# Prefix sums as rows of the second score product, pairs split at once, and a first batch in plain float32 products

## The chip, the cores and the metric

The kernel runs on one core of a Trainium2 chip. The metric is the device time of one execution in microseconds (us). Five engines matter: PE (TensorE, which multiplies; its weight loads are shown apart, as PEld), DVE (VectorE), ACT (ScalarE), POOL (GpSimd) and SP, which here only issues DMA transfers. Each engine takes its instructions strictly in the order in which the program has them.

## The reference

A forgetting attention feeds a channel mix. All is float32; 8 batches, 8 heads, 576 positions, 64 values a head.

```python
scores = q @ k.T / sqrt(64)
cum    = cumsum(maximum(s, 0))
bias   = -(cum[:, None] - cum[None, :])
scores = where(causal, -1e9, scores + minimum(bias, 0))
attn   = softmax(scores)
x      = attn @ v                      # heads side by side: 512 values a position
xk, xr = mix of x and the position before, by mu_k and mu_r
out    = sigmoid(xr @ w_r) * (relu(xk @ w_k) ** 2 @ w_v)
```

A row's own cumulated sum is the same for the whole row and falls out of the softmax, so the kernel adds only the sum of the key's position to a score.

## The kernel before, in words

**Products.** PE multiplies float32 operands at the rate of a rounded form (fp32r). To keep accuracy each operand is split in a high part (a cast by ACT) and a low part (a subtraction by POOL or DVE). For the scores, G holds the high part of q in rows 0 to 63 and the low part in rows 64 to 127; KH holds the high part of k twice, KL the low part twice. Two products into one PSUM bank, G by KH and G by KL, then hold all four partial products (line 689). For the values the weights are split in ph and pl and V holds high and low parts side by side (line 944); the two halves of the result are put together by ACT and DVE (lines 974 and 978).

**Tiles.** A head's queries come in five tiles: tile 0 of 64 queries and tiles 1 to 4 of 128, which see 64, 192, 320, 448 and 576 keys. For each tile: the two products, then DVE's pass at line 704, which adds the bias and scales, writes W and keeps the running minimum nm (one instruction and a read of its accumulator for each piece), then ACT's exponentials with their sums (722), POOL's division (736), transposes on PE (783, 797), and the split of the transposed weights (823 to 887). The bias of a tile comes from CB, a copy of the head's prefix sums on all 128 partitions that a DMA brings (629), and for the diagonal block from M, which POOL makes out of CB by an affine_select that puts -1e9 above the diagonal (649). So a tile's pass is cut at the diagonal block: a head of all five tiles has 10 pieces.

**Stages.** Heads are worked in pairs (a visit). Batch 0 is visited in two rounds: first tiles 0 to 2 of its four pairs (A), then tiles 3 and 4 (Z); the other batches take all five tiles in a visit (ALL). The result xT of a visit goes to DRAM (x_d, line 1272). The channel mix takes 256 positions of it at a time (a chunk, 36 in all, loaded at line 1173): lines 1020 to 1052 mix and split, 1081 and 1148 are the two large products, 1123 the gate. The weights arrive in float64 and are taken apart by ACT, DVE and POOL in the first 120 us (lines 506 to 537).

**Order.** A planner writes the order: every instruction is a task with an engine, a cost, what it depends on and a due time; `Plan.forward` puts them in a list for each engine. Loads of the next visit are due LEAD = 1.85 steps ahead, its split (`prepare`) 0.17 of a step behind the start of the visit before. Until the first value product, PE fills pauses with products of the identity (line 359). The change leaves the due times of the visits and chunks as they are; the order of nearly every engine is new all the same, since it comes out of the costs.

Of the kernel before, what the change touches and what calls it, by code (L numbers as in the profile page):

```python
# [285 lines left out]
def forgetting_attention_then_channel_mix(  # L286
# [15 lines left out]
    nc = tc.nc  # L302
# [94 lines left out]
    def zero(t):  # L397
        for kb in range(NQ - 1):
# [12 lines left out]
    cum_d = fixed(dram.tile([B * H, S], F32, name="cum_d"))  # L411

    def prefix_sums():
        cum = sbuf([B * H, S], "mask", 2)
        spos = sbuf([B * H, S], "mask", 2)
        ones = sbuf([B * H, S], "raw", 4)
# [19 lines left out]
        dma(lambda: nc.sync.dma_start(cum_d.ap, cum.get()), [cum], [cum_d], 410)  # L436

    def first_sums(nk):

        raw = sbuf([P, 2, nk], "raw", 4)  # L440
        ones = sbuf([P, nk], "raw", 4)
        cbs = [sbuf([P, nk], "cb", 2) for _ in range(2)]
        dma(
            lambda: nc.sync.dma_start(raw.get(), s[0:1, 0:2, 0:nk].broadcast_to([P, 2, nk])),
            [], [raw], 819 * 2 * nk / S,
        )
        pool(lambda: nc.gpsimd.memset(ones.get(), 1.0), [], [ones], nk, 36)
        act(
            lambda: nc.scalar.activation(raw.get(), raw.get(), AF.Relu, scale=ISCALE),
            [], [raw], 2 * nk, 94,  # L450
        )
        for j in range(2):
            dve(
                lambda j=j: nc.vector.tensor_tensor_scan(
                    out=cbs[j].get(), data0=ones.get(), data1=raw.get()[:, j], initial=0.0,
                    op0=ALU.mult, op1=ALU.add,
                ),
                [ones, raw], [cbs[j]], 2 * nk,
            )
        return cbs  # L460

# [83 lines left out]
    first = []  # L545
# [26 lines left out]
    def load_turned(src, b, hp, a, e, tag, plain):  # L572

        if plain:
            x = sbuf([P, e - a], tag, 3)
            dma(
                lambda: nc.sync.dma_start(
                    x.get(), src[b, 2 * hp : 2 * hp + 2, :, a:e].rearrange("h d t -> (h d) t")
                ),
                [], [(x, 0), (x, 1)], 819 * (e - a) / S,  # L580
            )
            return [x]
        xs = [sbuf([P, e - a], "raw", 4) for _ in range(2)]
        for j in range(2):
            for r in range(2):
                dma(
                    lambda j=j, r=r: nc.sync.dma_start(
                        xs[j].get()[64 * r : 64 * r + 64], src[b, 2 * hp + j, :, a:e]
                    ),
                    [], [(xs[j], r)], 410 * (e - a) / S,  # L590
                )
        return xs

    def split_qk(qs, ks):

        nq, nk = qs[0].n, ks[0].n
        G = [sbuf([P, nq], "G", 3, F32R) for _ in range(2)]
        KH, KL = ([sbuf([P, nk], x, 3, F32R) for _ in range(2)] for x in ("KH", "KL"))
        for j in range(2):
            k, kh, kl = ks[j], KH[j], KL[j]  # L600
            act(
                lambda k=k, kh=kh: nc.scalar.copy(kh.get(), k.get()),  # L602
                [(k, 0), (k, 1)], [(kh, 0), (kh, 1)], nk, 150,
            )
            pool(
                lambda k=k, kh=kh, kl=kl: nc.gpsimd.tensor_tensor(  # L606
                    out=kl.get(), in0=k.get(), in1=f32(kh.get()), op=ALU.subtract
                ),
                [(k, 0), (k, 1), (kh, 0), (kh, 1)], [(kl, 0), (kl, 1)], nk, 114, 2.21,
            )  # L610
            q, g = qs[j], G[j]
            act(
                lambda q=q, g=g: nc.scalar.copy(g.get(), q.get()),
                [(q, 0), (q, 1)], [(g, 0), (g, 1)], nq, 150,
            )
            pool(
                lambda q=q, g=g: nc.gpsimd.tensor_tensor(  # L617
                    out=g.get()[64:P], in0=q.get()[64:P], in1=f32(g.get()[64:P]), op=ALU.subtract
                ),
                [(q, 1)], [(g, 1)], nq, 114, 2.21,  # L620
            )
        return G, KH, KL

    def scores(b, h, tiles, G, KH, KL):

        NK = KN[tiles[-1]]
        CB = sbuf([P, NK], "cb", 2) if not first else first.pop(0)
        (b == 0 and h < 2 and tiles == A) or dma(
            lambda: nc.sync.dma_start(
                CB.get(), cum_d.ap[b * H + h : b * H + h + 1, 0:NK].broadcast_to([P, NK])  # L630
            ),
            [cum_d], [CB], 819 * NK / S,
        )
# [7 lines left out]
        M = sbuf([P, S], "mask", 2)  # L641

        def mask(m, k0, n):
            def own(x):
                x = x.get()[:m, k0 : k0 + n * m]
                return x if n == 1 else x.rearrange("p (t x) -> p t x", x=m)

            pool(
                lambda: nc.gpsimd.affine_select(
                    out=own(M),  # L650
                    in_=own(CB),
                    pattern=[[-1, m]] if n == 1 else [[0, n], [-1, m]],
                    base=0,
                    channel_multiplier=1,
                    compare_op=ALU.is_ge,
                    fill=MASK * ISCALE,
                ),
                [CB], [(M, k0 > 0)], n * m, 137,
            )

        def halved(t, a, x):
            return x.rearrange("p (k x) -> p k x", x=64) if lead(t) and a >= QS[t] else x

        def placed(t, a, e, x):
            if not lead(t):
                return x[:, a:e]
            if a < QS[t]:
                return x[:, 64 + a : 64 + e]
            x = x[:, : KN[t] // 64 * 64].rearrange("p (k x) -> p k x", x=64)
            return x[:, KN[t] // 64 - 1 :: 1 - KN[t] // 64]  # L670

        def products(t, m, i, k0, w, W):
            ps = bank(1, "s", 2)
            q0 = QS[t] - QS[tiles[0]]
            if KL is None:
                r = slice(64 * (h % 2), 64 * (h % 2) + 64)
# [3 lines left out]
                        G.get()[r, q0 : q0 + m],  # L680
                        KH.get()[r, k0 : k0 + w],
# [3 lines left out]
                    [(G, x) for x in range(2)] + [(KH, x) for x in range(2)], [ps], w, m, 4 / 2.4, 64,  # L685
                )
            for x, K in enumerate((KH, KL) if KL is not None else ()):
                pe(
                    lambda x=x, K=K: nc.tensor.matmul(  # L689
                        ps.get()[:m, :w],  # L690
                        G.get()[:, q0 : q0 + m],
                        K.get()[:, k0 : k0 + w],
# [3 lines left out]
                    [(G, x) for x in range(2)] + [(K, x) for x in range(2)], [ps], w, m,  # L696
# [651 lines left out]
```

## Time and profile before

| | us |
|---|---|
| median of 3 runs | 919.47 (918.21 to 920.49) |
| profiled execution | 918.27 |
| its span | 916.5 |
| PE busy | 861.8 (94%) |
| DVE busy | 714.7 (78%) |
| ACT busy | 702.1 (77%) |
| POOL busy | 519.1 (57%) |

The span is the time from the first to the last instruction. Busy shares are means over stages that differ: in the first 140 us the other engines are as full as PE, and PE's granted clock, 1.00 at 2.4 GHz, is lower there. PE's busy time counts each product up to its modelled end, and products overlap, so the pace of PE is read from starts.

### The profile page before, as it was taken

What the parts mean: (1) busy time and instruction counts of PE and PEld (TensorE: products, weight loads), DVE (VectorE), ACT (ScalarE), POOL (GpSimd) and SP (SyncE); (2) the same over time, 40 slices, a digit from 0 to 9 for tenths busy, and PEclk for the clock granted to TensorE, in tenths of its full rate; (3) what the DMA queues carried; (4) which work ended last, traced back from release to release, by engine and by line L of the source; (5) the groups of instructions that cost most, each with busy time, mean ns of one, the idle gap of its engine ahead of it and who ended that gap; (6) DMA issues with size and microseconds to landing.
All of it is one profiled execution on the core that took longest, in us unless ns stands there. A gap on an engine that the chain in (4) does not pass through costs nothing. (4 is left out here: it accounts for less than half of the span.)

```text
span 916.5 us, 18293 instructions
## 1 busy us (share of the span) xinstructions
PE 861.8 (94%) x5354; PEld 746.7 (81%) x5354; DVE 714.7 (78%) x2537; ACT 702.1 (77%) x1906; POOL 519.1 (57%) x880
## 2 busy tenths in 40 slices
PE   6778789999999999999999999999999999998998
PEld 4557667877888888897989898989798979888886
DVE  5998998988988888788878888888887877546431
ACT  5888888989998889688978888888787977445331
POOL 6998788698776566666663747564566552100000
PEclk7568979999999999999999999999999999999999
DMA  7788835446355342534342525242435220101100
GB/s 207 219 230 253 237 99 170 115 133 181 112 149 166 104 146 87 145 105 154 111 140 86 158 92 154 76 146 86 139 105 152 80 74 25 41 31 35 47 24 24
DMA packets 65044, 110.87 MB, mean 121 GB/s; under 512 B 10544, under 2 KB 26416, under 8 KB 64944
## 3 DMA queue, kind: packets, MB, share of 16 engines
q1 hardware_dynamic: 64944, 109.71, 40.5%
q8 instruction: 42, 0.69, 0.3%
q14 instruction: 58, 0.48, 0.2%
HBM read 90.64 MB, written 19.04 MB: 120 GB/s over the span
## 5 line engine op out<-in xcount | busy, mean ns | idle before, releaser
L1081 PE MATMUL m<-xh,w_k 128*128 128x256 f32 x1152 | 231.4, 286 | 2.8 <-DVE kl L1110 2.5
L722 ACT ACTIVATE W<-W,nm 128x448 f32<-128x448 f32 (+4 forms) x320 | 179.7, 562 | 44.0 <-DVE nm L704 40.8
L1148 PE MATMUL m<-w_v,kh 128*128 128x512 f32 x576 | 197.4, 400 | 0.0
L1081 PEld LDWEIGHTS m<-xh,w_k 128*128 128x128 f32 x1152 | 186.4, 190 | 5.2 <-DVE kl L1110 3.1
L736 POOL TENSOR_SCALAR W<-W,rinv 128x192 f32<-128x192 f32 (+4 forms) x320 | 165.4, 537 | 19.3 <-DVE rinv L766 17.4
L1081 PE MATMUL m<-xl,w_k 128*128 128x256 f32 x576 | 163.1, 283 | 0.0
L689 PE MATMUL s<-KH,G 128*128 128x288 f32 (+4 forms) x384 | 124.8, 333 | 19.0 <-DVE nm L704 13.9
L617 POOL TENSOR_TENSOR G<-raw,G 64x576 fp32r<-64x576 f32 (+2 forms) x72 | 93.1, 1293 | 76.3 <-issue 50.8
L825 DVE TENSOR_TENSOR pl<-t,ph 128x256 fp32r<-128x256 f32 (+3 forms) x264 | 120.1, 475 | 12.7 <-ACT ph L823 10.3
L606 POOL TENSOR_TENSOR KL<-raw,KH 128x576 fp32r<-128x576 f32 (+1 forms) x72 | 98.6, 1371 | 49.4 <-ACT KH L602 45.0
L783 PE MATMUL t<-ident,W 128*128 128x128 f32 x640 | 117.4, 285 | 8.2 <-POOL xT L1288 2.7
L1148 PEld LDWEIGHTS m<-w_v,kh 128*128 128x128 f32 x576 | 107.2, 189 | 17.7 <-ACT g L1135 0.2
L689 PE MATMUL s<-KL,G 128*128 128x288 f32 (+4 forms) x384 | 117.3, 308 | 1.1 <-POOL KL L606 1.1
L1029 DVE SCALAR_TENSOR_TENSOR xp<-x,mu,xp 128x256 f32<-128x256 f32 (+3 forms) x192 | 80.8, 421 | 45.9 <-ACT xp L1020 42.5
L944 PE MATMUL po<-ph,V 128*128 128x448 f32 (+4 forms) x344 | 106.9, 325 | 9.4 <-ACT ph L823 5.4
L823 ACT CAST ph<-t 128x256 fp32r<-128x256 f32 (+3 forms) x264 | 103.9, 417 | 14.3 <-PE t L783 6.0
L1148 PE MATMUL m<-w_v,kl 128*128 128x512 f32 x288 | 114.2, 397 | 0.0
L1081 PEld LDWEIGHTS m<-xl,w_k 128*128 128x128 f32 x576 | 109.2, 190 | 1.2 <-DVE xl L1052 0.4
L1020 ACT ACTIVATE xp<-x,mu 128x256 f32<-128x256 f32 (+3 forms) x192 | 81.4, 424 | 33.2 <-DVE xl L1052 11.1
L689 PEld LDWEIGHTS s<-KH,G 128*128 128x128 f32 (+1 forms) x384 | 72.3, 189 | 41.4 <-DVE nm L704 26.9
L704 DVE CUSTOM_DVE_ANT_0 W<-s,cb 128x64 f32<-128x64 f32 (+3 forms) x256 | 95.1, 376 | 11.6 <-PE s L689 9.9
L1123 PE MATMUL m<-w_r,xh 128*128 128x512 f32 x288 | 101.4, 407 | 0.1
(100 smaller groups left out, 1825.5 us busy)
## 6 DMA issues: line engine op xcount, KB each, us to landing
raw<-in_k SPq DMA_DIRECT2D x128, 144.0 KB, 3.1
cb<-cum_d SPq DMA_DIRECT2D x64, 288.0 KB, 3.8
raw<-in_q SPq DMA_DIRECT2D x112, 144.0 KB, 3.3
vn<-in_v SPq DMA_DIRECT2D x32, 320.0 KB, 3.4
out<-g SPq DMA_DIRECT2D x36, 256.0 KB, 2.4
x_d<-xT SPq DMA_DIRECT2D x28, 288.5 KB, 2.7
x<-x_d SPq DMA_DIRECT2D x12, 514.0 KB, 4.4
w_k<-in_moe_w_k SPq DMA_DIRECT2D x8, 512.0 KB, 5.2
```

The costliest lines, as they stand in the source:

```text
L606: lambda k=k, kh=kh, kl=kl: nc.gpsimd.tensor_tensor(out=kl.get(), in0=k.get(), in1=f32(kh.get()), op=ALU.subtract),
L689: lambda x=x, K=K: nc.tensor.matmul(ps.get()[:m, :w], G.get()[:, q0 : q0 + m], K.get()[:, k0 : k0 + w], start=x == 0, stop=x == 1,),
L704: lambda a=a, e=e, bias=bias, i=i: nc.vector.tensor_tensor_reduce(out=placed(t, a, e, W.ap[:m]), in0=halved(t, a, ps.get()[:m, a - k0 : e ...
L722: lambda: nc.scalar.activation(W.ap[:m, :n], W.ap[:m, :n], AF.Exp, bias=nm.get()[:m, 3 * t + mi : 3 * t + mi + 1], scale=-1.0, accum_out=s ...
L736: lambda: nc.gpsimd.tensor_scalar(out=to, in0=W.ap[:m, :n], scalar1=rinv.get()[:m, t : t + 1], scalar2=1.0, op0=ALU.mult, op1=ALU.mult,),
L783: lambda: nc.tensor.transpose(ps.get()[0:m, place : place + P], pt[t].ap[:, lead(t) + k0 : lead(t) + k0 + m], ident.ap),
L823: act(lambda: nc.scalar.copy(strips(ph), src()), [ps], [(ph, k) for k in ks], n * m)
L825: lambda: nc.vector.tensor_tensor(out=strips(pl), in0=src(), in1=f32(strips(ph)), op=ALU.subtract),
L944: lambda: nc.tensor.matmul(po.get()[: P if both else 64, at + q0 - base : at + q0 - base + m], V.get()[:, kb, 2 * j : 2 * j + (2 if both e ...
L1081: lambda u=u, f=f, c=c, n=n, w=w, x=x: nc.tensor.matmul(ps.get()[:, u * CT : (u + 1) * CT], weight["k", c, f // 4].get()[:, w, f % 4 * P : ...
L1123: lambda c=c, n=n, x=x, w=w: nc.tensor.matmul(ps.get(), x.get()[:, c, ts], weight["r", c, 0].get()[:, w], start=c == 0 and n == 0, stop=c ...
L1148: lambda f=f, n=n, x=x, w=w: nc.tensor.matmul(ps.get(), x.get()[:, f, ts], weight["v", f, 0].get()[:, w], start=f == 0 and n == 0, stop=f ...
```

## The change

**Batch 0.** `PLAIN = 8` makes its eight visits plain: q and k are loaded pair-wise as they are (`load_plain`) in rows 0 to 63, row 64 of k's tile gets the prefix sums and row 64 of q's a one, and one float32 product of 65 rows gives scores with their bias. V is not split, the weights are not split, one float32 product of 128 rows stands for two, and ACT alone copies the result.

**The other batches.** The prefix sums are cut in three fp32r pieces and put in rows 64 to 66 of KL, beside the low part of k in rows 0 to 63; the rest is zero. The second product has its own stationary operand, G2: the high part of q (a DMA copies it from G), three rows of ones, zeros. The first product is the old one. What CB and M did is now in the product, but for the mask, which is one constant tile (`causal`) for all heads. A tile's pass is cut only where its result is put in another order (tiles 2 and 4) and where a tile has two banks (tile 4): 8 pieces instead of 10. The second product gives up low q by low k.

**Pairs.** q and k of both heads are loaded and split by one instruction each.

```diff
+    def constant_rows():
+        for x in KLs + G2s:
+            dve(lambda x=x: nc.vector.memset(f32(x.get()[64:P]), 0.0), [], [(x, 1)], S)
+        for x in G2s:
+            dve(lambda x=x: nc.vector.memset(f32(x.get()[64 : 64 + PIECES]), 1.0), [], [(x, 1)], S)
...
+        dma(lambda: nc.sync.dma_start(whole_d.ap, cum.get()), [cum], [whole_d], 410)
+        first_cum.append(cum)
+        load(0)
+        plan.due = 15000.0
+        for i in range(PIECES):
+            dve(
+                lambda i=i: nc.vector.tensor_copy(sums_of_s.get()[:, i], cum.get()),
+                [cum], [(sums_of_s, i)], S,
+            )
...
+                    lambda j=j: nc.sync.dma_start(
+                        x.get()[64:65, j], first_cum[0].get()[row + j : row + j + 1, a:e]
+                    ),
...
+            dma(
+                lambda: nc.sync.dma_start(
+                    f32(KL.get()[64 : 64 + PIECES, :, 0:nk]),
+                    cum_d.ap[row : row + 2, :, 0:nk].rearrange("h p t -> p h t"),
+                ),
+                [cum_d, (KL, 1)], [(KL, (j, 2)) for j in range(2)], 520,
+            )
...
+                dma(
+                    lambda: nc.sync.dma_start(f32(G2.get()[0:64, :, 0:nq]), f32(G.get()[0:64])),
+                    part(G, 0), part(G2, 0), 819 * nq / S,
+                )
...
-        CB = sbuf([P, NK], "cb", 2) if not first else first.pop(0)
-        (b == 0 and h < 2 and tiles == A) or dma(
-            lambda: nc.sync.dma_start(
-                CB.get(), cum_d.ap[b * H + h : b * H + h + 1, 0:NK].broadcast_to([P, NK])
-            ),
-            [cum_d], [CB], 819 * NK / S,
-        )
...
-            if KL is None:
-                r = slice(64 * (h % 2), 64 * (h % 2) + 64)
+            if G2 is None:
                 pe(
                     lambda: nc.tensor.matmul(
                         ps.get()[:m, :w],
-                        G.get()[r, q0 : q0 + m],
-                        KH.get()[r, k0 : k0 + w],
+                        G.get()[0:65, h % 2, q0 : q0 + m],
+                        KH.get()[0:65, h % 2, k0 : k0 + w],
                         start=True,
                         stop=True,
                     ),
...
-            for a, e in ((k0, min(k0 + w, QS[t])), (max(k0, QS[t]), k0 + w)):
+            n = KN[t]
+            for a, e in ((k0, min(k0 + w, n - lead(t))), (max(k0, n - lead(t)), k0 + w)):
...
-                        in1=halved(t, a, bias.get()[:m, a:e]),
+                        in1=causal.get()[:m, S - P - QS[t] + a : S - P - QS[t] + e],
...
-        if 0 in tiles:
-            mask(64, 0, 1)
-        mask(P, QS[max(1, tiles[0])], len([t for t in tiles if t]))
...
+            if plain:
+                return
             dve(
                 lambda: nc.vector.tensor_tensor(
                     out=strips(pl), in0=src(), in1=f32(strips(ph)), op=ALU.subtract
                 ),
...
-    PLAIN, PLAINQ = 0, 0
+    PLAIN = 8
...
-    nc = bacc.Bacc("TRN2", target_bir_lowering=False, num_devices=1)
+    nc = bacc.Bacc("TRN2", target_bir_lowering=False, num_devices=1, dynamic_dma_scratch_size=1024)
```

Three places in the order of the program show what moves. PE in the early round of batch 0 before: value products of one head (po, by ph and pl), with the score products (s) of another head, two of each.

```order
L944 MATMUL po_87<-ph_103,V_174 128x320
L944 MATMUL po_87<-pl,V_174 64x320
L944 MATMUL po_87<-ph_103,V_174 128x192
L944 MATMUL po_87<-pl,V_174 64x192
L944 MATMUL po_87<-ph_103,V_174 128x64
L689 MATMUL s_205<-KH_276,G_248 128x320
L689 MATMUL s_205<-KL_288,G_248 128x320
L944 MATMUL po_87<-pl,V_174 128x64
```

The same engine and round after:

```order
L975 MATMUL po_93<-ph_120,V_217 128x320
L975 MATMUL po_93<-ph_120,V_217 128x192
L975 MATMUL po_93<-ph_120,V_217 128x64
L827 MATMUL t_313<-ident,W_72 128x128
L723 MATMUL s_203<-KH_190,G_102 128x320
L723 MATMUL s_201<-KH_190,G_102 128x192
```

One product in float32 stands where two in fp32r stood; the transposes (t) are what they were.

DVE in a head of all five tiles before: tiles 1 to 3 of the score pass (the rows with W; each is followed by the read of its accumulator), each in a piece with cb and one with mask (tile 3's second reads as tile 1's).

```order
L704 ISA W_72,nm_267<-s_208,cb_158 128x64
...
L704 ISA W_72,nm_267<-s_208,mask_105,nm_267 128x128
...
L704 ISA W_72,nm_267<-s_205,cb_158 128x192
L704 ISA nm_267 128x1
L704 ISA W_72,nm_267<-s_205,mask_105,nm_267 128x2x64
...
L704 ISA W_72,nm_267<-s_208,cb_158 128x320
```

The same tiles after:

```order
L751 ISA W_72,nm_232<-s_203,causal 128x192
L751 ISA nm_232 128x1
...
L751 ISA W_72,nm_232<-s_201,causal 128x256
...
L751 ISA W_72,nm_232<-s_201,causal,nm_232 128x64
...
L751 ISA W_72,nm_232<-s_203,causal 128x448
```

Tiles 1 and 3 have one piece instead of two, tile 2 still has two.

SP in the later batches after: the pieces of the sums (KL), the copy of q's high part (G into the second operand), and what is queued behind.

```order
L653 DMA KL_79<-cum_d 3x2x576
L1220 DMA x_649<-x_d_84 128x4x257
L635 DMA raw_97<-in_k 64x2x576 x2
L1324 DMA x_d_85<-xT_128 128x577
L576 DMA vn_867<-in_v 128x640
L698 DMA G_81<-G_819 64x1152
L635 DMA raw_99<-in_q 64x2x576 x2
```

Two loads of cb on 128 partitions for each pair are gone from this queue.

## Rows read from the trace of the kernel before

**Rows 1.** Windows by stage: length, busy us (instructions) of each engine, granted clock, DMA.

```profile
core 0: us, PE busy (x) PEld busy (x) DVE busy (x) ACT busy (x) POOL busy (x), PEclk, DMA share, GB/s
...
10.90:69.70 58.80, 43.20 (x169) 30.54 (x170) 51.81 (x197) 46.56 (x147) 53.53 (x97) 0.57 0.77 221
69.70:139.60 69.90, 59.08 (x334) 48.94 (x333) 64.85 (x207) 60.41 (x151) 58.38 (x76) 0.85 0.68 197
139.60:300.00 160.40, 152.34 (x1002) 131.08 (x1001) 140.76 (x562) 144.47 (x414) 122.50 (x210) 1.00 0.50 144
300.00:800.00 500.00, 490.95 (x3186) 435.47 (x3186) 403.71 (x1481) 403.36 (x1106) 279.33 (x474) 1.00 0.37 110
```

**Rows 2.** Timeline of SP, first two chunk loads: start, us, what.

```profile
69.73 0.59 SPq L1173 DMA_DIRECT2D x<-x_d  x1
...
140.24 0.56 SPq L1173 DMA_DIRECT2D x<-x_d  x1
```

**Rows 3.** Timeline of PE in the middle, two products back to back.

```profile
423.41 0.40 PE L1148 MATMUL m<-w_v,kl 128*128 128x512 f32 x1
423.64 0.62 PE L1148 MATMUL m<-w_v,kh 128*128 128x512 f32 x2
```

**Rows 4.** Timeline of PE in the early round.

```profile
31.88 0.47 PE L689 MATMUL s<-KH,G 128*128 128x320 f32 x1
32.15 0.47 PE L689 MATMUL s<-KL,G 128*128 128x320 f32 x1
...
33.47 0.69 PE L783 MATMUL t<-ident,W 128*128 128x128 f32 x2
33.95 0.42 PE L797 MATMUL t<-ident,W 128*128 128x128 f32 x1
```

**Rows 5.** Groups of DVE, 0 to 139.6 us: busy us, mean ns, idle before.

```profile
L825 DVE TENSOR_TENSOR pl<-t,ph 128x256 fp32r<-128x256 f32 (+2 forms) x40 | 16.0, 415 | 1.8 <-ACT ph L869 0.8 <-ACT ph L823 0.8
...
L978 DVE TENSOR_TENSOR xT<-po,xT 64x320 f32<-64x320 f32 (+1 forms) x16 | 7.2, 453 | 0.5 <-ACT xT L974 0.2
...
L875 DVE TENSOR_TENSOR pl<-t,ph 64x64 fp32r<-64x64 f32 x24 | 5.1, 213 | 0.2
```

**Rows 6.** Groups of ACT, 0 to 139.6 us.

```profile
L602 ACT CAST KH<-raw 128x576 fp32r<-128x576 f32 (+1 forms) x20 | 11.6, 582 | 0.7 <-DMA raw<-in_k 0.7
L613 ACT CAST G<-raw 128x320 fp32r<-128x320 f32 (+2 forms) x20 | 9.5, 475 | 0.0
```

**Rows 7.** Timeline of the start.

```profile
1.50 0.57 POOL L421 MEMSET raw<- 64x576 f32 x1
...
7.05 1.32 DVE L430 TENSOR_TENSOR_SCAN mask<-raw,mask 64x576 f32<-64x576 f32 x1
...
10.90 0.39 PE L689 MATMUL s<-KH,G 128*64 128x64 f32 x2 [3.30 <-POOL mask L649]
```

**Rows 8.** DMA issues: count, KB each, median us to landing.

```profile
cum_d<-mask SPq DMA_DIRECT2D x1, 144.0 KB, 2.4
```

**Rows 9.** Groups of the score pass, 139.6 us to the end, shapes apart.

```profile
L704 DVE CUSTOM_DVE_ANT_0 W<-s,mask,nm 128x128 f32<-128x128 f32 x218 | 74.9, 346 | 4.5 <-POOL sums L636 0.2 <-POOL rinv L761 0.2
L704 DVE DVE_READ_ACCUMULATOR2_ANT nm<- 128x1 f32 x490 | 40.2, 82 | 0.0
L704 DVE CUSTOM_DVE_ANT_0 W<-s,cb 128x320 f32<-128x320 f32 x54 | 26.2, 485 | 1.3 <-PE s L689 0.9
...
L704 DVE CUSTOM_DVE_ANT_0 W<-s,cb,nm 128x160 f32<-128x160 f32 x55 | 20.8, 378 | 2.0 <-PE s L689 0.7
L704 DVE CUSTOM_DVE_ANT_0 W<-s,cb 128x192 f32<-128x192 f32 x54 | 19.0, 353 | 4.3 <-PE s L689 3.8
L704 DVE CUSTOM_DVE_ANT_0 W<-s,cb 128x64 f32<-128x64 f32 x54 | 11.7, 216 | 2.7 <-PE s L689 2.2
```

**Rows 10.** Waits of PE's weight loads, 138 to 860 us: total, times, longest.

```profile
PEld s L689 <- DVE nm L704: 13.7, 30, 1.3
PEld po L944 <- DVE pl L825: 8.0, 16, 0.8
```

More of the change, by code (lines that the diff above doesn't have):

```diff
@@ L408, in forgetting_attention_then_channel_mix, with constants @@
     weight = {}
-    cum_d = fixed(dram.tile([B * H, S], F32, name="cum_d"))
+    PIECES = 3
+    sums_of_s = sbuf([B * H, PIECES, S], "kh", 1, F32R)
+    cum_d = fixed(dram.tile([B * H, PIECES, S], F32, name="cum_d"))
+    whole_d = fixed(dram.tile([B * H, S], F32, name="whole_d"))
+    first_cum = []
+    causal = fixed(const.tile([P, S], F32, name="causal"))
+    KLs = [fixed(const.tile([P, 2, S], F32R, name=f"KL{i}")) for i in range(2)]
+    G2s = [fixed(const.tile([P, 2, S], F32R, name=f"G2{i}")) for i in range(2)]
+    turns = [0]
+    def constants():
+        pool(lambda: nc.gpsimd.memset(causal.get(), 0.0), [], [causal], S, 36)
+        pool(
+            lambda: nc.gpsimd.affine_select(
+                out=causal.get()[:, S - P : S],
+                in_=causal.get()[:, S - P : S],
+                pattern=[[-1, P]],
+                base=0,
+                channel_multiplier=1,
+                compare_op=ALU.is_ge,
+                fill=MASK * ISCALE,
+            ),
+            [], [causal], P, 137,
+        )
[4 more added lines that the diff above has]
+            dve(lambda x=x: nc.vector.memset(f32(x.get()[64 : 64 + PIECES]), 1.0), [], [(x, 1)], S)
     def prefix_sums():
-        cum = sbuf([B * H, S], "mask", 2)
-        spos = sbuf([B * H, S], "mask", 2)
-        ones = sbuf([B * H, S], "raw", 4)
+        both, ones = sbuf([B * H, 2, S], "raw", 2), sbuf([B * H, S], "raw", 2)
+        cum, spos = Buffer(lambda: both.get()[:, 0]), Buffer(lambda: both.get()[:, 1])
+        cum.last = spos.last = None
+        cum.use = spos.use = both.use
         dma(
@@ new lines, in split_qk, with part @@
+    def split_qk(q, k, b, hp, apart):
+        nq, nk = q.n // 2, k.n // 2
+        G = sbuf([P, 2, nq], "G", 2, F32R)
+        KH = sbuf([P, 2, nk], "KH", 2, F32R)
+        KL, G2 = KLs[turns[0] % 2], G2s[turns[0] % 2]
+        turns[0] += 1
+        row = b * H + 2 * hp
+        if not apart:
+            dma(
+                lambda: nc.sync.dma_start(
+                    f32(KL.get()[64 : 64 + PIECES, :, 0:nk]),
+                    cum_d.ap[row : row + 2, :, 0:nk].rearrange("h p t -> p h t"),
+                ),
+                [cum_d, (KL, 1)], [(KL, (j, 2)) for j in range(2)], 520,
+            )
+        for js in ((0, 1), (1, 2)) if apart else ((0, 2),):
+            c = slice(*js)
+            n = js[1] - js[0]
+            def part(x, r, js=js):
+                return [(x, (j, r)) for j in range(*js)]
+            if apart:
+                dma(
+                    lambda j=js[0]: nc.sync.dma_start(
+                        f32(KL.get()[64 : 64 + PIECES, j, 0:nk]),
+                        f32(sums_of_s.get()[row + j : row + j + 1, :, 0:nk]),
+                    ),
+                    [(sums_of_s, i) for i in range(PIECES)] + [(KL, 1)], [(KL, (js[0], 2))], 520,
+                )
+            act(
+                lambda c=c: nc.scalar.copy(KH.get()[:, c], k.get()[:, c]),
+                part(k, 0) + part(k, 1), part(KH, 0), n * nk, 150,
@@ L638, in scores @@
         pt = list(pt) + [bases[h % 2], KO[NQ - 1] if tiles == A and h % 4 > 1 else 0]
[L641 to L670, printed above, removed]
         def products(t, m, i, k0, w, W):
```

177 lines of the change are left out of this document (94 added, 83 removed).

## The prediction

> **What bounds the kernel now.** I read the windows by stage first, to find where TensorE is not the limit, then the waits of TensorE in the long middle, then the timeline for what one product costs at either clock, and last the groups of instructions that the change touches.
>
> The windows [rows 1] show three regimes. From 139.6 to 800 us PE is busy 152.3 of 160.4 and 491.0 of 500 us at a granted clock of 1.00: TensorE sets the pace there. Before, it does not. In 10.9 to 69.7 us (the early tiles 0 to 2 of batch 0, which I call stage A) the clock is 0.57 and POOL (53.5 of 58.8), DVE (51.8) and ACT (46.6) are all nearly full. In 69.7 to 139.6 us (the late tiles 3 and 4 of batch 0, beside the first chunk of the mix: stage Z) DVE is busy 64.9 of 69.9, ACT 60.4, POOL 58.4, at a clock of 0.85. The limits of the two stages are the loads of the first two chunks, at 69.73 and 140.24 us [rows 2]. What comes after batch 0 is a fixed store of PE work, so a stage that ends earlier moves the end of the kernel by the same time, as long as PE does the same work in it.
>
> PE's busy time counts the fill of the pipeline, so I count work by starts. At full clock a product of 512 columns starts 0.23 us after the last one [rows 3]: 0.449 ns a column. In stage A, 320 columns take 0.27 us from start to start [rows 4]: 0.84 ns, the lower level of 1.2 GHz. Two transposes start within 0.48 us there [rows 4]: 0.24 each, so 0.12 at full clock.
>
> **Part 1: batch 0 in float32 products, no splits.** Batch 0 has 8 A heads (576 score and 576 value columns each) and 8 Z heads (1024 and 1024): 9,216 and 16,384 columns in 48 and 64 products. Before, each is streamed twice. No row shows a float32 product. The bounds: one pass, as the float32 transposes [rows 4]; or four passes each with a weight load that nothing hides. I take four hidden passes, since the old code gets the four partial products of two split operands in two passes only by stacking both parts of q in 128 rows, or both parts of V in 128 columns, and the new operands are not stacked. Then A streams 9,216 x 4 x 0.449 = 16.6 us and Z 29.4, together 46 where it was 23: **PE gets 23 us more work**, at full clock.
>
> The Trainium skill ("FP8 and Floating Point Precision", TensorE Precision Notes) says that true float32 takes four passes through the array. By it the sum is the one above, and nothing in the trace of before can confirm it.
>
> What goes on the other engines, in the stretch to 139.6 us: on DVE the low parts of the weights, the two additions of value parts, 16.0 + 7.2 + 5.1 = 28.3 us [rows 5] and two small groups that I leave out. On ACT 16 of the 20 casts of k and of q belong to batch 0: 0.8 x (11.6 + 9.5) = 17 us [rows 6]; the casts of V come on top. POOL loses the low parts of q, k and V and the masks, and has the most room of all.
>
> The stages then hold:
> - A: DVE 51.8 less 15 (the share of A's heads in the 28.3, and part 2) plus 2.5 for five 64x576 passes that make the pieces of the sums (the fill of that size took 0.57 [rows 7]) = 39; ACT 46.6 - 9 = 38; PE 16.6 + 32 transposes x 0.12 = 20 at full clock, and with a clock midway between 0.57 and 1.00 about 26. The longest is DVE. POOL was 91% of this stage; with chains of three engines I take 87% for DVE: **45 us instead of 58.8**.
> - Z: DVE 64.9 - 18 = 47, ACT 60.4 - 8 = 52; PE 29.4 + 64 x 0.12 + the first chunk without the later part of its output (by the code 96 products of 256 columns, 24 of 512 for the gate and half of the 48 of 512 for the output, 22 us) = 59 at full clock, which I take since PE has hardly a pause then. PE becomes the bound. At the 95% of 139.6 to 300 us [rows 1]: **62 us instead of 69.9**.
>
> Together 107 for 128.7: -21.7.
>
> **The start.** The first product came at 10.90 us, after the mask on POOL [rows 7]. Now DVE first issues two fills of 640 and four of 1152 elements (the code's constant rows), then the scale of s, one more fill, and the scan of 1.32 us [rows 7]; at POOL's 0.57 us for 576 that is 0.7 + 1.3 + 4.6 + 0.5 + 1.1 + 1.3 = 9.5 us, and a copy of one row inside SBUF, whose nearest row is the store of the sums with 2.4 us to landing [rows 8], plus its issue: 12.4, so +1.5. Were DVE's fills free it would be -0.7. Behind that copy SP holds the loads of the second visit, which the first visit's two heads cover.
>
> **Part 2: constant mask, bias as rows.** Each head of the later batches has 8 score passes on DVE instead of 10. Without a running minimum the pieces take 216, 353 and 485 ns for 64, 192 and 320 columns, about 1.05 ns a column; with it 346 and 378 for 128 and 160; each is followed by a read of 82 [rows 9]. Tile 1 goes from 216 + 346 + 82 to 353 (-0.29), tile 3 from 485 + 346 + 82 to some 617 (-0.30); tiles 2 and 4 keep their number of pieces and their time. That is 0.59 us a head, 33 us of DVE over 56 heads; POOL loses its masks. The second product streams as many columns as before, with three rows of sums in place of copies. None of this is on PE, so it is worth what PE waits: of 13.7 us for the score passes and 8.0 for the low parts [rows 10] I take half and a quarter: **-9**. Bounds: 0, where the waits have other ends, and -22, where all goes.
>
> **Part 3: pairs at once.** One cast for two heads saves a fixed part on ACT and POOL that PE does not see: 0. New on SP is the copy of q's high part for the second product; it waits for ACT's cast, and behind it stand stores of x_d, the loads of the next pair and of V. They are issued a visit ahead (LEAD is 1.85 steps), which hides a landing of a few us; I cost it at 0, and a rival takes the other case.
>
> **Sum**, against the profiled execution of 918.3 us (its span of 916.5 and 1.8 around it): -21.7 + 1.5 - 9 = -29.2, 889.1. The median of the runs shown is 1.2 above that execution, so about **890 us**.
>
> **Rivals.**
> - *The clock stays* at 0.57 and 0.85. For: PE still waits in A. Against: twice the streaming. A stays at 45 (PE 20 / 0.57 = 36), Z is 59 / 0.85 / 0.95 = 73: -10.7 + 1.5 - 9, **901 us**.
> - *One pass.* PE's Z work falls by 22 us to 37, and ACT bounds Z with 52 / 0.9 = 58: -25.7 + 1.5 - 9, **886 us**. For: the float32 transposes run so [rows 4]. Against: they multiply by ones and zeros only.
> - *Slower: the passes pay their loads.* Place: PE in batch 0. With the 0.12 us of a transpose for each of 4 loads, A gains 23 and Z 31 us of PE: A 43 / 0.78 / 0.87 = 64, Z 90 / 0.95 = 95, together 159 for 128.7: +30.3 + 1.5 - 9, **942 us**. It decides from an average of about 0.89 us a product in Z (I have 29.4 / 64 = 0.46). Against: 256 columns or more hide a load in every pass of before.
> - *Slower: the copy on SP is late.* If half of a 2.4 us landing shows in each of the 28 later visits, that is 34 us: **924 us**. It decides from 1 us a visit, 28 in all. Against: the visit ahead.
>
> **How the numbers follow.** Forecast 0.62, with its own range 877 to 903 (bounds 0 and -22 of the middle, and 5 us in either stage); clock stays 0.16; one pass 0.08; loads 0.08; late copy 0.06. The range of 870 to 912 leaves out the two slow rivals and little else. About 0.3% can be told from no change here, 2.8 us. Faster: the first three, and a part of the fourth's milder cases, 0.88; slower 0.09; within 0.3% 0.03.
>
> **What would show it.** Right: the loads of the first chunks near 58 and 121 us, a clock near 1.00 in stage Z with PE as its busiest engine, 320-column float32 products about 0.6 us apart, the first product near 12.4 us, and fewer waits of PE for score passes after batch 0. Wrong: float32 products of 0.9 us and more, PE waiting for the second product's stationary operand in later visits, a second chunk that loads after 140 us, or a middle in which PE waits as long as before for others.

## The result, and the profile after

The changed kernel takes **897.84 us** (median of 4 runs, 896.33 to 900.30) where the one before took 919.98 beside it (918.21 to 922.15): a ratio of 0.976, 95% interval 0.973 to 0.979. The forecast was 890, with a range of 870 to 912. The profiled execution took 897.21, its span is 895.2, the mean granted clock 0.992.

I split the span at the second chunk load, as the prediction did: the **head** up to it, and the **stretch** from it to the end, in which PE has the same work in both kernels.

| us | before | forecast | after |
|---|---|---|---|
| first product | 10.9 | 12.4 | 12.15 |
| first chunk load | 69.7 | 58 | 53.1 |
| second chunk load | 140.2 | 121 | 113.7 |
| stretch from there to the end | 776.3 | 9 less | 781.5 |

So the head gave 26.5 us and the stretch took 5.2 back. The engines over the whole span, from the page (busy us, share, instructions):

```profile
PE 853.7 (95%) x5356; PEld 740.3 (83%) x5356; DVE 675.0 (75%) x2196; ACT 676.0 (76%) x1809; POOL 416.6 (47%) x646
```

The windows by stage, cut at the new loads, with the columns of [rows 1]:

```profile
core 0: us, PE busy (x) PEld busy (x) DVE busy (x) ACT busy (x) POOL busy (x), PEclk, DMA share, GB/s
12.20:53.10 40.90, 36.84 (x170) 25.21 (x171) 38.97 (x134) 35.04 (x126) 25.14 (x54) 0.88 0.80 241
53.10:113.70 60.60, 57.42 (x331) 47.83 (x330) 50.23 (x136) 52.22 (x131) 39.16 (x47) 0.98 0.62 173
113.70:300.00 186.30, 177.47 (x1147) 153.34 (x1146) 156.39 (x575) 165.36 (x456) 118.63 (x180) 1.00 0.49 126
300.00:800.00 500.00, 487.90 (x3163) 432.88 (x3162) 380.43 (x1275) 386.47 (x1031) 230.57 (x345) 1.00 0.35 96
```

Stage A (first row) is 40.9 us long and DVE is busy in 38.97 of them; stage Z (second row) is 60.6 and PE is busy in 57.4, at a clock of 0.98. The last two rows can't be laid beside those of [rows 1], since the changed kernel is 26 us ahead in its work by then. So here is the stretch whole, before and after:

```profile
140.24:916.50 776.26, 752.86 (x4815) 662.29 (x4813) 591.99 (x2125) 589.90 (x1600) 401.20 (x683) 1.00 0.35 105
113.72:895.20 781.48, 753.92 (x4823) 663.09 (x4821) 575.72 (x1915) 585.92 (x1550) 349.18 (x525) 1.00 0.35 95
```

The gain of the masks and biases is there, 16.3 us of DVE and 52.0 of POOL. PE is busy as long as before, within 1.1 us, and yet the stretch is 5.2 longer: PE idles more. The loads that end the stages, on SP (start, us, what), to be read against [rows 2]:

```profile
53.12 0.56 SPq L1220 DMA_DIRECT2D x<-x_d  x1
...
113.72 0.56 SPq L1220 DMA_DIRECT2D x<-x_d  x1
```

The timeline of PE in batch 0 shows what a float32 product costs; its count at the end of a row (x2) is one product, since each shows as two records:

```profile
12.15 0.45 PE L723 MATMUL s<-KH,G 65*64 65x64 f32 x2 [4.90 <-DMA KH<-raw]
...
33.61 0.70 PE L723 MATMUL s<-KH,G 65*128 65x320 f32 x2
34.15 0.28 PE L827 MATMUL t<-ident,W 128*128 128x128 f32 x1
...
62.37 0.65 PE L723 MATMUL s<-KH,G 65*128 65x288 f32 x2
62.86 1.13 PE L975 MATMUL po<-ph,V 128*128 128x256 f32 x4
```

320 columns hold PE 0.54 us (33.61 to 34.15) and 288 columns 0.49, where one pass at the 0.449 ns a column of [rows 3] would take 0.144 and 0.129: 3.8 passes, so four with the loads hidden. The forecast's "about 0.6 us apart" was four passes. The Trainium skill's four passes ("FP8 and Floating Point Precision", TensorE Precision Notes) agree with these rows.

The waits of PE's weight loads from 114 to 860 us (total, times, longest), against [rows 10]:

```profile
PEld s L734 <- DVE nm L751: 22.2, 30, 1.6
PEld po L991 <- ACT ph L867: 7.2, 11, 1.7
PEld po L991 <- DVE pl L871: 5.2, 12, 1.0
```

The wait for the low parts fell, 8.0 to 5.2. The wait for the score passes did not fall; it rose from 13.7 to 22.2. This row is the one that the experiments are about: a score product needs a PSUM tile that DVE's last pass has left.

### The profile page after: what moved, and what is told of

It reads as the page before. It is cut to its first block, busy times and chain, and to the rows that moved or that the text cites. A ratio compares the mean times of both kernels' runs of the same rounds, so it can differ in the third digit from the quotient of the medians.

```text
span 895.2 us, 16954 instructions
## 1 busy us (share of the span) xinstructions
PE 853.7 (95%) x5356; PEld 740.3 (83%) x5356; DVE 675.0 (75%) x2196; ACT 676.0 (76%) x1809; POOL 416.6 (47%) x646
## 4 chain that ended last, share of the span: by engine, by line
PE 52%; DVE 19%; ACT 19%; issue 5%; DMA 3%; POOL 1%; ACTq 0%; DVEq 0%; POOLq 0%; SPq 0%
PE m L1128 17%; PE m L1195 11%; PE m L1170 6%; PE s L734 5%; PE po L991 5%; ACT W L769 4%; DVE xp L1076 4%; DVE W L751 4%; ACT xp L1067 4%; PE t L827 4%; DMA x<-x_d 3%; ACT ph L867 3%; DVE pl L871 2%; DVE xT L1025 2%; PE po L975 2%
## 5 line engine op out<-in xcount | busy, mean ns | idle before, releaser
L783 POOL TENSOR_SCALAR W<-W,rinv 128x576 f32<-128x576 f32 (+4 forms) x320 | 165.0, 536 | 37.5 <-DVE rinv L810 31.7
L751 DVE CUSTOM_DVE_ANT_0 W<-s,causal 64x64 f32<-64x64 f32 (+4 forms) x320 | 127.9, 409 | 25.5 <-PE s L734 18.3
L871 DVE TENSOR_TENSOR pl<-t,ph 128x512 fp32r<-128x512 f32 x224 | 104.1, 485 | 20.1 <-ACT ph L867 18.1
L734 PE MATMUL s<-KH,G 128*64 128x64 f32 x336 | 102.2, 312 | 12.7 <-DVE nm L751 12.4
L702 POOL TENSOR_TENSOR G<-raw,G 64x1152 fp32r<-64x1152 f32 x28 | 74.9, 2676 | 58.2 <-issue 47.4
L734 PE MATMUL s<-KL,G 128*64 128x64 f32 x336 | 98.3, 295 | 0.0
L867 ACT CAST ph<-t 128x512 fp32r<-128x512 f32 x224 | 88.8, 426 | 11.2 <-PE t L827 5.6
L827 PEld LDWEIGHTS t<-ident,W 128*128 128x128 f32 x640 | 79.5, 141 | 17.8 <-DVE pl L871 3.6
L991 PE MATMUL po<-ph,V 128*128 128x448 f32 x280 | 84.5, 318 | 3.9 <-ACT ph L867 3.4
L734 PEld LDWEIGHTS s<-KH,G 128*64 128x64 f32 x336 | 60.3, 180 | 29.3 <-DVE nm L751 24.1
```

The costliest lines, as they stand in the source:

```text
L734: lambda x=x, g=g, K=K: nc.tensor.matmul(ps.get()[:m, :w], g.get()[:, h % 2, q0 : q0 + m], K.get()[:, h % 2, k0 : k0 + w], start=x == 0, s ...
L751: lambda a=a, e=e, at=at, i=i: nc.vector.tensor_tensor_reduce(out=W.ap[:m, at : at + e - a], in0=ps.get()[:m, a - k0 : e - k0], in1=causal ...
L783: lambda: nc.gpsimd.tensor_scalar(out=to, in0=W.ap[:m, :n], scalar1=rinv.get()[:m, t : t + 1], scalar2=1.0, op0=ALU.mult, op1=ALU.mult,),
L827: lambda: nc.tensor.transpose(ps.get()[0:m, place : place + P], pt[t].ap[:, lead(t) + k0 : lead(t) + k0 + m], ident.ap),
L871: lambda: nc.vector.tensor_tensor(out=strips(pl), in0=src(), in1=f32(strips(ph)), op=ALU.subtract),
L991: lambda: nc.tensor.matmul(po.get()[: P if both else 64, at + q0 - base : at + q0 - base + m], V.get()[:, kb, 2 * j : 2 * j + (2 if both e ...
```

## The experiments

For each kernel the table gives the median, and from its profiled run the second chunk load, the stretch from there to the end, and the total of the wait in the row above (PEld's s for DVE's nm) in that stretch. The kernel before, beside them, had medians of 917.67 to 919.11.

| kernel | median | second load | stretch | wait |
|---|---|---|---|---|
| before | 919.98 | 140 | 776 | 13.7 |
| p1_only | 914.31 | 131 | 779 | 14.5 |
| p2_only | 931.30 | 148 | 781 | 21.6 |
| after | 897.84 | 114 | 781 | 22.2 |
| ten_pieces | 915.45 | 119 | 792 | 33.1 |
| double_late | 912.02 | 128 | 782 | 22.1 |
| rows64 | 911.83 | 128 | 781 | 21.5 |
| per_head | 904.79 | 115 | 787 | 24.0 |
| cast_for_copy | 901.07 | 115 | 785 | 23.0 |
| rows_on_pool | 895.48 | 119 | 784 | 21.2 |
| ten_planned | 906.31 | 118 | 786 | 26.0 |
| real_cost | 897.57 | 126 | 772 | 11.2 |
| other_order | 900.38 | 117 | 782 | 21.6 |
| real_cost_late | 890.73 | 113 | 776 | 12.8 |

### The parts alone

**p1_only**: the kernel before, with batch 0 in float32 products and nothing else.

```diff
...
-    PLAIN, PLAINQ = 0, 0
+    PLAIN, PLAINQ = 8, 8
```

> Part 1 alone: the kernel before, with the first batch in float32 products of 64 rows, the weights not split and V not split there; prefix sums still come as copies on 128 partitions and the diagonal blocks are still made on POOL for every head. Theory: the whole gain of the change is made in the first batch, because DVE, POOL and ACT are relieved there, so this one takes 895 to 902 us, with the loads of the first two chunks near 54 and 116 us (after the change 53.1 and 113.7, before 69.7 and 140.2). Rival: the constant mask and the rows of sums carry half of it, then 906 to 912 us.

Measured 914.31, ratio 0.996 (0.994 to 0.998): hardly any gain, and slower than both cases expected. The windows of its early round (columns as above) show why:

```profile
20.00:30.00 10.00, 10.00 (x29) 6.05 (x27) 9.12 (x35) 7.49 (x26) 7.61 (x19) 0.50 0.79 271
30.00:40.00 10.00, 10.00 (x29) 6.42 (x28) 8.91 (x34) 7.34 (x25) 7.49 (x18) 0.50 0.82 270
40.00:50.00 10.00, 10.00 (x28) 6.38 (x27) 8.34 (x26) 7.48 (x26) 6.21 (x15) 0.50 0.70 236
```

PE's records fill all the time, at 1.2 GHz, and no wait of PE shows there, so PE is itself the limit. The part by itself is the forecast's rival "the clock stays". Its score products have 64 rows, since the sums still come as copies; rows64 below takes that up. In the changed kernel, the same round at 20 to 50 us:

```profile
20.00:30.00 10.00, 9.13 (x51) 6.64 (x50) 9.38 (x44) 8.78 (x35) 5.86 (x16) 0.92 0.81 242
30.00:40.00 10.00, 9.84 (x52) 7.08 (x51) 9.58 (x38) 9.56 (x40) 7.26 (x20) 1.00 0.85 261
40.00:50.00 10.00, 9.53 (x47) 6.34 (x46) 9.43 (x28) 9.81 (x32) 6.38 (x11) 1.00 0.73 225
```

There the clock is back near 2.4 GHz within the first of these windows, and PE, DVE and ACT are all nearly full.

**p2_only**: the changed kernel with split products in batch 0 too; the constant rows and the pieces of the sums are then due at the very start, and the first load stands behind the sums. One fill of KL comes at 28.94 us, behind the store of the sums in it at 24.64, so this kernel leaves out the bias of the first visit.

```diff
...
-    PLAIN = 8
+    PLAIN = 0
...
-    plan.due = 25000.0
+    plan.due = -2900.0
```

> Parts 2 and 3 alone: the changed kernel with no plain visits, so the first batch too is split, with its sums as rows of the second product and the constant mask. Theory: the middle is not limited by DVE or POOL, and what it is relieved of there is worth nothing; the first batch loses its masks on POOL and 5 us of DVE, so 912 to 920 us (before 920). Rival: the 9 us that were forecast for the middle are there, and something in batch 0 took them away again: 903 to 911 us.

Measured 931.30, ratio 1.014 (1.012 to 1.016), slower than both cases expected. But its first product comes only at 25.8 us, behind POOL's split of q, so the head says nothing on the change. Its stretch does: 781 us and a wait of 21.6, as after the change, where p1_only has 779 and 14.5, nearer to the kernel before. What raised the wait came with parts 2 and 3 and the order drawn for them, not with the float32 products.

### Is a shorter pass worth anything?

**ten_pieces**: the passes of tiles 1 and 3 cut at the diagonal, as before the change; every engine's order stays that of the changed kernel.

```diff
...
+                    if t in (1, 3):
+                        piece(a, QS[t], at, low, 3 * t + 2)
+                        piece(QS[t], e, at + QS[t] - a, 3 * t + 2, 3 * t + i)
+                    else:
+                        piece(a, e, at, low, 3 * t + i)
...
```

> The changed kernel with the score pass of tiles 1 and 3 cut at the diagonal block as before, in the same order on every engine: 10 pieces a head instead of 8, that is about 0.59 us more DVE a head, 33 us in all over the later batches. Theory: DVE has room in the middle, so 896 to 901 us, as the change. Rival: the middle did gain from the shorter pass and lost it elsewhere, then 905 to 915 us here.

Measured 915.45, ratio 0.996 (0.994 to 0.998). The stretch grew by 10.2 us and the wait by 10.9 (first the stretch, with the columns of the windows above, then the wait):

```profile
119.22:910.90 791.68, 760.06 (x4823) 662.54 (x4821) 597.65 (x2133) 589.17 (x1552) 348.30 (x525) 1.00 0.34 94
PEld s L734 <- DVE nm L751: 33.1, 53, 1.9
```

DVE is busy 21.9 us more than in the changed kernel, so in a fixed order the stretch pays about half of what DVE takes longer; my theory that it would not care fell. The rest of the median's 17.6 us is in the head, where tiles 1 and 3 are cut too and the profile has a clock of 0.50 from 20 to 30 us. **ten_planned** has the same cut, and the planner knows of it:

```diff
...
+            cut = QS[t] if t in (1, 3) else n - lead(t)
+            for a, e in ((k0, min(k0 + w, cut)), (max(k0, cut), k0 + w)):
...
```

> The changed kernel with the score pass of tiles 1 and 3 cut at the diagonal again (10 passes a head on DVE instead of 8), as in the kernel ten_pieces, but now the planner is told, so the order on all engines is drawn for 10 passes. With the order of 8 passes the two extra passes cost 10 us between the second chunk load and the end (791.7 against 781.5). Theory A, the planner takes any length of pass into account: drawn for 10 passes the stretch is back near 782 (778 to 786), so a shorter pass by itself was never worth anything here; median about 898 to 906. Theory B, the length of the passes is real work on the path: the stretch stays near 790 (787 to 794), median about 907 to 915, and something else in the change has cost those 10 us.

906.31, ratio 0.987 (0.985 to 0.988), stretch 786.1, wait 26.0. That lies between the two theories: an order drawn for the two passes hides about half of their 10 us.

### Does the clock or PE hold the head?

**double_late**: in stage Z each score product is issued twice, 13.7 us more of PE at full clock.

```diff
...
+                    for _ in range(2 if tiles == Z else 1):
...
```

> The changed kernel with each score product of the late tiles of the first batch (3 and 4) issued twice into the same bank: 8 heads x 1024 columns x 4 cycles, 13.7 us more PE work between the loads of the first and second chunk, same order otherwise. Theory: PE is the bound of this stage, so 907 to 912 us and a second chunk load 9 to 14 us later. Rival: ACT and DVE are its bound and PE waits, then 898 to 902 us.

912.02, ratio 0.992 (0.990 to 0.994). The second chunk load came 14.4 us later, near the 13.7. Stage Z went from 60.6 to 65.4 us, PE busy in 63.5 of them: PE bounds Z, but only 4.8 us show there. The rest is in stage A, which ended 10 us later, for two reasons that this run does not part: some of the doubled products already ran in it (84 records of score products for 66), and the clock was 0.50 and 0.52 in the windows from 20 to 40 us of the profiled run. One of its runs, at a mean clock of 0.991, took 909.58, about 12 more than the changed kernel at 0.992; how that divides I can't say without its profile.

**rows64**: the plain score products over 64 rows instead of 65. The bias of batch 0 is left out by this; the order of all else stays.

```diff
-                        G.get()[0:65, h % 2, q0 : q0 + m],
-                        KH.get()[0:65, h % 2, k0 : k0 + w],
+                        G.get()[0:64, h % 2, q0 : q0 + m],
+                        KH.get()[0:64, h % 2, k0 : k0 + w],
```

> The changed kernel with the first batch's score products over 64 rows instead of 65, same order on every engine; the row of prefix sums, and so the bias of the first batch, is left out. It asks why the early round is short after the change (41 us at a granted clock of 0.87) and not with float32 products alone (0.61, first chunk load at 68 us, PE busy 46 of 48 us). Theory: it is the granted clock, and a product of 64 rows does not bring it back as one of 65 rows does; then clock under 0.75 in the early round, first chunk load at 60 to 68 us, 905 to 914 us. Rival: the row count does nothing and the difference lies in the order and in the masks on POOL; then 896 to 901 us with the load near 53.

911.83, ratio 0.992 (0.989 to 0.995): 14 us more than with 65 rows. The stretch is unchanged (781.5), so it is all in the head: the first chunk load came at 64.8 us, and the clock from the first product to there was 0.71 where it was 0.88, as my theory had it. Eight runs at clocks of 0.979 to 0.981 took 911.5 to 912.7, one at 0.974 took 916.66, and one at 0.996 took 900.22.

**rows_on_pool**: the fills of the constant rows go from DVE to POOL.

```diff
-            dve(lambda x=x: nc.vector.memset(f32(x.get()[64:P]), 0.0), [], [(x, 1)], S)
+            pool(lambda x=x: nc.gpsimd.memset(f32(x.get()[64:P]), 0.0), [], [(x, 1)], 2 * S, 36)
...
```

> The changed kernel with the fills of constant rows on POOL instead of DVE, so that DVE's scan of the prefix sums does not stand behind six of them. Theory: the first product comes at 9 to 10.5 us instead of 12.2 and the whole kernel ends 1 to 3 us earlier, 894 to 897 us. Rival: the early round is limited by the weights and the clock, and the start is worth nothing: 897 to 900 us.

895.48, ratio 0.978 (0.973 to 0.983). Three runs at a clock of 0.988 took 894.8 to 895.7; the fourth, the profiled one, at 0.977 took 905.17. There the first product came at 10.8 us, and yet:

```profile
20.00:30.00 10.00, 10.00 (x34) 7.57 (x33) 6.29 (x27) 6.95 (x29) 4.76 (x14) 0.50 0.64 185
30.00:40.00 10.00, 10.00 (x30) 7.11 (x30) 6.14 (x25) 4.77 (x18) 4.27 (x10) 0.50 0.44 129
40.00:50.00 10.00, 10.00 (x31) 7.24 (x30) 5.71 (x21) 6.27 (x28) 3.51 (x9) 0.51 0.44 124
```

One program has two outcomes 10 us apart, and the mean clock goes with them. Only the longer run has a profile; there the clock stays at 1.2 GHz for 30 us. Beside that an earlier first product counts for little: the median is 2.4 us under the changed kernel's, but the ratio to the kernel before is no better (0.978 and 0.976).

### Pairs, and the copy on SP

**per_head**: in the later batches each head's q and k split by instructions of their own.

```diff
-        for js in ((0, 1), (1, 2)) if apart else ((0, 2),):
+        for js in ((0, 1), (1, 2)):
...
```

> The changed kernel with the splits of q and k made for each head by itself in the later batches: two casts, two subtractions of 576 instead of one of 1152, two copies. It asks what took back in the middle what the shorter score pass gives (the middle from the second chunk load to the end is 781.5 us after the change and 776.2 before, while two pieces a head more cost some 13 us). Theory: the whole-pair splits, 2.7 us each on POOL, and the late release of their buffers hold up heads; then 886 to 893 us. Rival: they do not; then 895 to 902 us, a little slower for the fixed parts.

904.79, ratio 0.988 (0.984 to 0.993), stretch 787.3. That is slower than both cases expected. The pairs do not hold the stretch up; undoing them costs some 6 us, part of which may be the new order.

**cast_for_copy**: G2's high part of q by a second cast on ACT, without the copy on SP.

```diff
-            if apart:
+            if True:
```

> The changed kernel with the second operand's high part of q made by a second cast on ACT instead of a DMA from the first. Theory: the copy on SP comes late or holds back the loads behind it; then 886 to 894 us in spite of some 1.2 us more on ACT for each of 28 pairs. Rival: the copy is hidden and ACT, at 92% between 130 and 260 us, pays; then 899 to 908 us.

901.07, ratio 0.982 (0.980 to 0.985), stretch 785.0. Without the copy nothing is faster, though ACT has 26 us more to do here. The trace of the changed kernel settles it: from 113 us to the end no wait of PE or of its weight loads ends with that copy, so it was hidden.

### The plan's price of a pass

The passes of the stretch after the change, shapes apart (busy, mean ns of one, idle before), as in [rows 9]:

```profile
L751 DVE CUSTOM_DVE_ANT_0 W<-s,causal 128x448 f32<-128x448 f32 x55 | 34.0, 618 | 3.1 <-PE s L734 2.5
...
L751 DVE CUSTOM_DVE_ANT_0 W<-s,causal,nm 128x64 f32<-128x64 f32 x110 | 30.6, 279 | 1.6
```

By its formula (columns / 0.96 + 68 ns) the planner holds the first for 535 ns and the second for 135. **real_cost** adds 160 ns to the planner's price of every pass; the instructions are the same, and only their order changes.

```diff
-                    [(W, i), (nm, (t, i))], e - a,
+                    [(W, i), (nm, (t, i))], e - a + 154,
```

> The changed kernel in which the planner's cost of a score pass on DVE is raised by 160 ns, to about what the trace shows (448 columns: 618 ns and a read of 82, against 535 in the plan; 64 columns: 278 and 82, against 135); nothing else is edited, so only the order changes. Theory C, the order drawn with too short passes sends PE to a score tile before DVE has left it (PE's wait for nm in 200 to 800 us is 29.8 us after the change and 13.7 before): the wait falls under 20 us, the stretch from the second chunk load to the end falls from 781.5 to 768 to 776, and the median to 884 to 892. Rival D, the waits are not due to the plan's costs: the stretch stays at 778 to 786, the wait at 25 or more, the median at 895 to 902. A rise over 902 would say that the plan's other costs are tuned around the short ones.

The stretch fell to 772.0, and the wait with it (the idle time of PE and of PEld before score products with nm as releaser, added, was 15.9 us from 200 to 800 us, where it was 29.8):

```profile
PEld s L734 <- DVE nm L751: 11.2, 18, 1.7
```

The median, 897.57 (ratio 0.976, 0.974 to 0.978), did not move and missed the 884 to 892 expected, since the order of batch 0 was drawn anew too and its second load came at 126 us. **real_cost_late** raises the price in the later batches alone:

```diff
+                    [(W, i), (nm, (t, i))], e - a + (0 if G2 is None else 154),
```

> The kernel real_cost, with the planner's cost of a score pass raised by 160 ns in the later batches only; the passes of batch 0 keep the short cost. The whole order is drawn anew, so this is a second, different order drawn with real costs. Theory C (PE reached score tiles that DVE had not left, since the plan held the passes for too short): from the second chunk load to the end 768 to 776 again (781.5 after the change, 772.0 in real_cost), PE's wait for nm in 200 to 800 us under 20 us (29.8 and 15.9). Rival G (real_cost was one lucky order): 778 to 788, the wait at 22 or more. If the head goes as after the change (second chunk load at 114 us; it was 126 in real_cost) the span is near 886 and the median 886 to 891, faster than both kernels; if the head goes as in real_cost, the median is 894 to 900.

Second load at 113, stretch 775.7, median **890.73**, ratio 0.972 (0.969 to 0.974): the fastest version here. By the medians that is 7 us under the changed kernel; by the ratios, each to the kernel before beside it, it is 4, and the two intervals overlap a little. Its row:

```profile
PEld s L734 <- DVE nm L751: 12.8, 19, 1.6
```

Both orders drawn with the higher price have the short wait; the five orders drawn with the low one for the same eight passes (p2_only, after, per_head, cast_for_copy and rows_on_pool) have 21.2 to 24.0. ten_planned, at the low price too, has 26.0. Theory C holds for the eight passes.

**other_order** was meant as a control for the draw of an order: one of the planner's gaps at 155 ns for 150.

```diff
-    SELF = {"PE": 0.0, "ACT": 150.0, "DVE": 127.0, "POOL": 62.0, "SP": 0.0}
+    SELF = {"PE": 0.0, "ACT": 155.0, "DVE": 127.0, "POOL": 62.0, "SP": 0.0}
```

> A control: the changed kernel with one of the planner's gaps, ACT behind ACT, at 155 ns instead of 150; the work is the same, only the order drawn is another. It says how far the stretch from the second chunk load to the end (781.5) and the time (897.8) move by the draw of the order alone. Theory E, the draw matters little: stretch 778 to 785, median 894 to 902. Rival F, the draw is worth as much as what is disputed here: a stretch off by 6 us or more either way (under 775 or over 788), a median under 892 or over 905; then the 5.3 us that the middle lost, and the 10 us of ten_pieces, cannot be put down to the work of the change from single kernels.

900.38, ratio 0.979 (0.977 to 0.982), stretch 781.7. But the order came out almost the same, so this is a repeat and no control: it shows that one order repeats its stretch within 0.5 us (after, other_order, rows64 and double_late have 781.5 to 781.9), while the head varies. Its clock came back later than in the changed kernel's profile, which had 0.92 in this window, and its first chunk load came at 55.6 us instead of 53.1:

```profile
20.00:30.00 10.00, 9.76 (x35) 6.88 (x34) 6.67 (x30) 6.02 (x24) 4.43 (x12) 0.57 0.67 197
```

How far a mere draw moves the stretch stays unmeasured.

## Why the prediction was right, and where it was not

The mechanism of the head was right, the total came out 8 us too low, and two errors stood against each other: the head gave 7 us more than forecast, the middle 14 less. That the total came so near is in part luck.

- **The price of a float32 product**: four hidden passes, as taken. The rivals with one pass and with paid loads fall with the same rows. What spoke for one pass was misread: two transposes in 0.48 us [rows 4] are 0.24 us for 128 columns, 1.9 ns a column, more than two passes at the 0.84 there.
- **The start**: +1.25 us for +1.5. A fill of 1152 took 1.02 us where 1.1 was estimated; the timeline of DVE (start, us):

```profile
2.37 1.02 DVE L439 MEMSET KL<- 64x1152 f32 x1 [0.19 <-issue]
...
8.84 1.35 DVE L461 TENSOR_TENSOR_SCAN raw<-raw,raw 64x576 f32<-64x576 f32 x1
```

- **Stage A**: DVE's 39 us of work came out as 38.97, though not term by term: four of the five passes that make the pieces of the sums took 4.1 us in the stage, where all five were put at 2.5. The stage took 40.9 and not 45: the mis-sized term is the share, 87% by guess, 95% measured.
- **Stage Z**: forecast 62 us bounded by PE at 95% of 59; measured 60.6 with PE busy 57.4, 95%.
- **The rival "the clock stays"** did not come true here, but it does in kernels one step away: p1_only has mean clocks of 0.965 to 0.974 in all ten runs, rows64 was low in nine of ten, rows_on_pool in one of four. The changed kernel's four runs lie between 0.987 and 0.992. That it fell on the better side is luck as far as the forecast goes, which named no reason for the clock to return but "twice the streaming"; p1_only has that too.
- **The middle: this step failed.** "None of this is on PE, so it is worth what PE waits": half of the wait for the score passes and a quarter of that for the low parts, -9, with bounds of 0 and -22. The low parts went as forecast (8.0 to 5.2). The wait for score passes rose by 8.5, and the stretch by 5.2. The step took the waits of before as a stock that a lighter DVE can only draw on. They depend on the order, which was drawn anew, with a price of a pass that is too low by 80 to 150 ns: real_cost and real_cost_late show the wait at 11.2 and 12.8 when the same instructions are ordered by a higher price. And ten_pieces shows that within one order PE pays about half of what DVE's passes take longer. So a bound of 0 was too tight: a new order can lose.
- **The size of the saving on DVE** was wrong as well. I added the 82 ns of the read behind each piece, but in the rows below the read ends with its pass. The timeline of DVE after the change:

```profile
506.75 0.36 DVE L751 CUSTOM_DVE_ANT_0 W<-s,causal 128x192 f32<-128x192 f32 x1 [0.63 <-PE s L734]
507.03 0.08 DVE L751 DVE_READ_ACCUMULATOR2_ANT nm<- 128x1 f32 x1
507.07 0.42 DVE L751 CUSTOM_DVE_ANT_0 W<-s,causal 128x256 f32<-128x256 f32 x1
507.42 0.08 DVE L751 DVE_READ_ACCUMULATOR2_ANT nm<- 128x1 f32 x1
```

The read starts at 507.03, before the pass from 506.75 is over at 507.11. By [rows 9] without reads, tile 1 saves 216 + 346 - 351 = 211 ns and tile 3 485 + 346 - 618 = 213: 0.42 us a head, 24 us of DVE and not 33. (DVE's busy time in the stretch fell by less, 16.3, since neighbouring passes overlap in the records, as at 507.07.) My raise of 160 ns in real_cost was by the same error too high for long passes (535 + 160 for 618) and about right for the short chained ones (135 + 160 for 279).
- **Pairs** cost at 0: per_head puts them at up to 6 us of gain. **The copy on SP** at 0: right.

Open: why the order before, drawn with the same low price, had only 13.7 us of this wait; so why the wait rose is not shown, only that another order takes it away. The number of passes alone is not the reason, since ten_planned has ten and 26.0. The kernel before with the higher price was not run, so how much of the 6 to 10 us that real_cost gained in the stretch belongs to this change can't be told. How the head's 26.5 us divide between the lighter engines and the clock isn't shown either: with the clock low, p1_only had 9 of them and rows64, in the changed kernel's order, 12. Nor is it known what in a run decides when the clock returns.

## What to carry to other kernels

Where a planner draws the order, a lighter engine need not shorten the waits for it: put the measured duration of the instruction that releases the bound engine's buffers in the plan first, and give the term of such a change a bound on the side of loss. Split the span at a milestone, and compare stretches of equal work: here one number, the wait for one kind of buffer, roughly followed the stretch through fourteen kernels, while the medians were moved by the clock too. Moving work onto TensorE at the start gained little here where the clock stayed low (p1_only, 0.996); look at the granted clock in steps of 10 us, and at several runs.

## What was not expected of the hardware

- PE's records showed it busy for 10.00 of every 10 us from 20 to 50 us and the granted clock stayed at 0.50 (p1_only, and rows_on_pool in its profiled run), while the changed kernel had 0.92 from 20 to 30 with PE busy 9.13. By their mean clocks, runs of one program (rows_on_pool, rows64) went either way.
- Score products over 64 rows instead of 65, in the same order but without the bias of batch 0, left the mean clock at 0.979 to 0.981 in eight of ten runs, against 0.987 to 0.992: 912 us for 898. Products over 65 rows had the low clock too in the profiles of rows_on_pool and double_late, so the row count alone does not decide.
- A float32 product shows as two records, each of about the time of two passes: the four records in the row at 62.86 us are two products of 256 columns, and two of the records start at 63.18 and 63.39 us, 0.21 apart, where one pass is 0.115 at 0.449 ns a column.
- The accumulator's read cost DVE nothing behind its pass in the rows at 507 us: it starts some 80 ns before the pass's recorded end.
